# A second batch whose query factors are divided by their sums before the split, with the order of all instructions made anew

## The chip, the cores and the metric

The kernel runs on one core of a Trainium2 chip. Its metric is the device time of one execution in microseconds (us); the time before is the median of three runs. The engines are named as in the profile: PE (TensorE, matmuls) with its weight loads PEld, DVE (VectorE), ACT (ScalarE), POOL (GpSimd) and SP (SyncE, which here only issues transfers).

## What is computed

For each of 4 batches with 12608 tokens of 128 channels, 49 agents attend to the tokens (`a2k`), the tokens attend to the agents (`q2a`), and an expert network is added for the 128 tokens of a batch with the highest scores:

```python
a2k = sm(agents, k)                 # softmax(agents k^T / sqrt(128))
agent_v = a2k @ v                   # 49 x 128
q2a = sm(q, agents)                 # e / (e.sum(-1) + 1e-9), e = exp(s - max)
x = q2a @ agent_v
scores = x @ w_gate
top = the 128 highest scores of the batch
out[top] = x[top] + sigmoid(scores[top]) * (relu(x[top] @ w1) @ w2)   # w1: 128 x 1024
```

All other rows of the output are `x`.

## The kernel before

A batch is cut into 7 chunks of 15 columns of 128 tokens (the last has 9). For each chunk the kernel loads keys, values and queries by one transfer each (960 KB, 967.5 KB and 960 KB) and stores one chunk of outputs.

- Keys (`k_front`): PE multiplies agents and keys in fp32 into score banks `S` (3 of them), DVE transposes a bank into `sk` and takes its maxima `mx`. When all 7 chunks are there, `k_max` finds the batch's maxima `mb`; `k_exp` subtracts them (POOL) and takes the exponential (ACT); `v_tiles` sums with the values on PE (`av`); `v_finish` makes the fp16 weights `ws` in two halves, and `iv`, which undoes their scale.
- Queries (`q_scores`): scores as before, transposed by DVE into `sq`, with the maximum `qm` of each token. `q_exp` subtracts (POOL) and takes the exponential (ACT). `q_high` and `q_low` split it into two fp16 halves, the tile `f` (ACT, POOL). PE transposes `f` (`fT`), DVE or ACT copies that to `ft`, which is kept. PE then makes the gate scores from `ft` (`pg`), and `topk` finds the 128 rows.
- Outputs (`q_out`): PE multiplies `ft` by the two halves of `ws` into a bank `po` (4 columns at a time), and DVE, ACT or ACT and POOL bring it to `og`, which is stored. `TAIL` and `FILL` name the order in which the outputs are handed to the planner: batch 0, 1, 3, 2.
- The expert network (`expert`) runs for batches 0 to 2 as one group and for batch 3 alone. POOL gathers the rows, PE makes `qT`, `sc`, `eT`, `xT`, `xe`, the hidden layer `ph` (copied to `hT`) and the product `py`; DVE adds, and POOL scatters the rows `ey` into the output by an indirect transfer. A batch's scatter waits for all its stores.

A batch in `EARLY` is treated in another way: its exponentials are divided by their sum before they are split, so its outputs need only the constant `iv`:

```python
# q_exp, only for a batch in EARLY
nc.vector.tensor_reduce(m[:, :n], sv, axis=AX.X, op=ALU.add)
nc.scalar.activation(m[:, :n], m[:, :n], AF.Identity, scale=1.0 / FSCALE, bias=eps)
nc.vector.reciprocal(m[:, :n], m[:, :n])
# q_high, only for a batch in EARLY: one product on POOL (sq<-sq,qm a second time)
# q_out, modes A and V: for a batch in EARLY, then for another
nc.scalar.activation(o4, p3, AF.Copy, scale=d["iv"][:, 0:1])
nc.vector.tensor_scalar(o4, p3, d["iv"][:, 0:1], None, op0=ALU.mult)
nc.vector.tensor_tensor(o4, p3, rate.broadcast_to([P, nt, C]), op=ALU.mult)
# q_out, mode P: for a batch not in EARLY
nc.scalar.copy(o4, p3)
nc.gpsimd.tensor_tensor(o4, o4, rate.broadcast_to([P, nt, C]), op=ALU.mult)
```

For a batch outside `EARLY`, `q_rates` computes the rates `r` of its tokens from a third column of `pg`. `MODES` has one letter for each quarter of a chunk.

The order of the instructions is made by a planner (`place`) before anything is issued. It walks through time with a cost for each instruction, and where several are ready on an engine it takes the one with the lowest number in the table `RANKS`, less `STICK` if it is of the same kind as the last one on that engine. Each engine then works through its list in order. All instructions are issued in one place, so the profile gives them all line 1435; they are told apart by their tiles.

Of the kernel before, what the change touches and what calls it, by code (L numbers as in the profile page):

```python
# [40 lines left out]
EARLY = (0,)  # L41
MODES = ('AVAV', 'VPVP', 'VPVP', 'VPVP')
# [7 lines left out]
STICK = 6130.565386853517  # L50
# [242 lines left out]
def place(rec, urgency, slack=0.0, stick=0.0):  # L293
# [81 lines left out]
    ('setup', 0): {"ACT": -123995.537, "POOL": -226775.386, "DVE": -330989.174},  # L375
# [9 lines left out]
    ('kmax', 0): {"DVE": -300206.643, "PE": -380208.421},  # L385
    ('exp', 0, 0): {"POOL": 16775.417, "ACT": -716011.048},
    ('exp', 0, 1): {"POOL": 30570.947, "ACT": 1275522.702},
    ('exp', 0, 2): {"POOL": 35917.562, "ACT": -748687.739},
    ('exp', 0, 3): {"POOL": 36968.681, "ACT": -701284.356},
    ('exp', 0, 4): {"POOL": 100274.596, "ACT": 1572848.174},  # L390
    ('exp', 0, 5): {"POOL": -23068.358, "ACT": 2543086.262},
    ('exp', 0, 6): {"POOL": 583242.912, "ACT": 134593.062},
    ('v', 0, 0): {"SP": -505160.849},
    ('av', 0, 0): {"PE": 55332.469},
    ('v', 0, 1): {"SP": -28568.405},
    ('av', 0, 1): {"PE": 27249.223},
# [71 lines left out]
    ('qe', 1, 0): {"POOL": -369154.478, "ACT": 1570736.67},
    ('turn', 1, 0): {"PE": -325314.263, "ACT": 1886989.053},
    ('gate', 1, 0): {"PE": 38546.353},  # L470
    ('q', 1, 1): {"SP": 37927.979, "PE": 111380.947, "DVE": -12731.903},
    ('qe', 1, 1): {"POOL": -548476.653, "ACT": 255692.298},
    ('turn', 1, 1): {"PE": 209170.337, "ACT": 1551250.834},
    ('gate', 1, 1): {"PE": -375489.615},
    ('q', 1, 2): {"SP": 41692.369, "PE": -22703.96, "DVE": -11241.058},
    ('qe', 1, 2): {"POOL": -313899.94, "ACT": -1601627.448},
    ('turn', 1, 2): {"PE": -355624.568, "ACT": 955330.754},
    ('gate', 1, 2): {"PE": 620462.051},
    ('q', 1, 3): {"SP": 41757.771, "PE": 30839.917, "DVE": -227921.899},
# [5 lines left out]
    ('turn', 1, 4): {"PE": 8157.362, "ACT": 401148.205},
    ('gate', 1, 4): {"PE": -179875.682},
    ('q', 1, 5): {"SP": 43756.473, "PE": 18263.577, "DVE": 112204.08},
    ('qe', 1, 5): {"POOL": 19270.315, "ACT": 1762395.711},
    ('turn', 1, 5): {"PE": 31038.115, "ACT": 1850548.195},
    ('gate', 1, 5): {"PE": 63331.63},  # L490
    ('q', 1, 6): {"SP": 50286.516, "PE": -349161.909, "DVE": -12804.369},
# [211 lines left out]
def agent_attention_moe(ctx, tc, qT, kT, va, agT, wgb, w1, w2, consts, qs, outs, capacity):  # L703
# [810 lines left out]
```

## Time and profile before

| | |
|---|---|
| median of 3 runs | 294.15 us (293.65 to 295.35) |
| the profiled execution | 294.86 us, with a span of 293.0 us from first to last instruction |
| PE, DVE, ACT, POOL busy | 265.7 us (91%), 218.5 (75%), 169.9 (58%), 186.2 (64%) |
| moved by DMA | 106.68 MB, mean 364 GB/s |
| chain that ended last | PE 44% of the span; ACT 7%, DMA 7%, DVE 2% |

Times of the trace are counted from the span's start. Busy is the time in which an engine has an instruction under way. A releaser is the work that ended an engine's idle time. The chain of waits is followed back from the last instruction. A matmul in fp32 is recorded as two passes. A row by stretch has the stretch and its length, then each engine's busy time with its instructions in brackets, the clock granted to PE as a share of its full 2.4 GHz, the busy share of the 16 DMA engines, and what they moved.

### The profile page before, as it was taken

Reading aid. Unit: us, or ns where it says so; the run is one execution under the profiler, and the core shown is the slowest. Engines: PE = TensorE matmul, PEld = TensorE weight load, DVE = VectorE, ACT = ScalarE, POOL = GpSimd, SP = SyncE. Lnnn points to the kernel's source line nnn. Section 1 sums busy time; section 2 is a strip of 40 time slices with the busy share of each in tenths; the row PEclk is TensorE's granted clock in tenths of the full one; section 3 lists DMA queues with packets and bytes.
Section 4 is the critical chain, followed back from the end, with each engine's and each line's share of the span. In section 5 each row is a group of like instructions: output and inputs, shape, how many; then the busy total and the mean of one; then the engine's idle time right before and its main releaser. Section 6 shows DMA issues by size and latency. Waiting matters only on the chain.

```text
span 293.0 us, 8554 instructions
## 1 busy us (share of the span) xinstructions
PE 265.7 (91%) x3524; PEld 176.5 (60%) x3524; DVE 218.5 (75%) x507; ACT 169.9 (58%) x306; POOL 186.2 (64%) x158
## 2 busy tenths in 40 slices
PE   1767898998999999999999999989999999999980
PEld 0212355663676544465856356456887988999880
DVE  1799977968954999985798985768928499897520
ACT  1021355432652399968675589497998759755300
POOL 8014699357992446699522597799908475879622
PEclk9999999999999999999999999999999999999995
DMA  7999999999999999999999999999902389999971
GB/s 278 425 406 426 416 417 422 415 422 423 421 417 422 416 419 423 402 294 410 421 418 395 406 418 340 380 392 410 343 12 92 136 350 415 400 418 398 414 300 33
DMA packets 18204, 106.68 MB, mean 364 GB/s; under 512 B 2032, under 2 KB 3440, under 8 KB 18160
## 3 DMA queue, kind: packets, MB, share of 16 engines
q1 hardware_dynamic: 17760, 105.42, 89.2%
q8 instruction: 30, 0.49, 0.7%
q0 software_dynamic: 256, 0.52, 0.6%
q10 hardware_dynamic: 144, 0.13, 0.1%
q14 instruction: 14, 0.11, 0.1%
HBM read 79.85 MB, written 26.21 MB: 362 GB/s over the span
## 4 chain that ended last, share of the span: by engine, by line
PE 44%; ACT 7%; DMA 7%; DVE 2%; issue 2%; POOL 1%; POOLq 0%; DVEq 0%
PE po L1435 13%; PE S L1435 8%; PE av L1435 8%; DMA xT<-qT 7%; PE fT L1435 4%; PE ph L1435 3%; ACT gt L1435 2%; PE all L1435 2%; PE pg L1435 2%; PE py L1435 2%; ACT ft L1435 2%; ACT sq L1435 1%; POOL out L1435 1%; ACT f L1435 1%; DVE og L1435 1%
## 5 line engine op out<-in xcount | busy, mean ns | idle before, releaser
L1435 PE MATMUL S<-xT,ag_sb 128*32 128x480 f32 (+1 forms) x896 | 101.3, 560 | 16.3 <-DMA ag_sb<-agT 6.2
L1435 POOL TENSOR_TENSOR sq<-sq,qm 128x735 f32<-128x735 f32 (+1 forms) x35 | 47.8, 1366 | 54.5 <-DVE qm L1435 42.7
L1435 PEld LDWEIGHTS <-ft 128*128 128x128 f16 x1188 | 58.1, 97 | 18.3 <-issue 16.3
L1435 PEld LDWEIGHTS S<-xT,ag_sb 128*32 128x32 f32 x896 | 24.3, 110 | 54.2 <-issue 16.1
L1435 ACT COPY ft<-fT 128x896 f16<-128x896 f16 (+2 forms) x49 | 43.4, 900 | 20.3 <-PE fT L1435 20.2
L1435 PE MATMUL po<-ws,ft 128*128 128x128 f16 x792 | 53.2, 219 | 1.6 <-ACT og L1435 0.6
L1435 POOL TENSOR_TENSOR f<-sq,f 128x735 f16<-128x735 f32 (+1 forms) x28 | 42.8, 1529 | 16.1 <-issue 7.7
L1435 PE MATMUL av<-v,sk 128*64 128x129 f32 x792 | 50.5, 276 | 0.4 <-DMA v<-va 0.4
L1435 PEld LDWEIGHTS av<-v,sk 128*64 128x64 f32 x792 | 44.7, 136 | 8.8 <-issue 4.9
L1435 POOL TENSOR_TENSOR og<-og,r 128x512 f32<-128x512 f32 (+1 forms) x39 | 35.9, 941 | 20.1 <-ACT og L1435 19.9
L1435 POOL TENSOR_TENSOR sk<-sk,mb 128x735 f32<-128x735 f32 (+1 forms) x28 | 47.1, 1701 | 0.6 <-DVE rs L1435 0.6
L1435 DVE STREAM_TRANSPOSE sq<-S 128x480 f32<-128x480 f32 (+1 forms) x56 | 35.7, 645 | 14.5 <-PE S L1435 11.5
L1435 DVE STREAM_TRANSPOSE sk<-S 128x480 f32<-128x480 f32 (+1 forms) x56 | 35.6, 639 | 9.3 <-PE S L1435 7.0
L1435 DVE TENSOR_REDUCE mx<-S 128x1 f32<-128x480 f32 (+1 forms) x56 | 33.4, 607 | 5.7 <-PE S L1435 5.2
L1435 DVE TENSOR_TENSOR og<-po,r 128x512 f32<-128x512 f32 (+1 forms) x42 | 27.0, 658 | 8.5 <-PE po L1435 7.1
L1435 PEld LDWEIGHTS <-f 128*128 128x128 f16 x396 | 22.9, 98 | 13.6 <-issue 8.9
L1435 DVE TENSOR_REDUCE qm<-sq 128x15 f32<-128x735 f32 (+1 forms) x35 | 30.2, 862 | 1.1 <-ACT sq L1435 0.7
L1435 ACT ACTIVATE sq<-sq,lift 128x735 f32<-128x735 f32 (+1 forms) x28 | 25.0, 893 | 9.5 <-POOL sq L1435 9.2
L1435 PE MATMUL fT<-idh,f 128*128 128x128 f16 x396 | 28.7, 220 | 0.5 <-ACT ft L1435 0.4
L1435 ACT CAST f<-sq 128x735 f16<-128x735 f32 (+1 forms) x28 | 22.2, 794 | 11.1 <-POOL sq L1435 10.9
L1435 ACT ACTIVATE sk<-sk 128x735 f32<-128x735 f32 (+1 forms) x28 | 22.2, 797 | 10.4 <-POOL sk L1435 10.3
L1435 ACT COPY og<-po 128x512 f32<-128x512 f32 (+1 forms) x39 | 20.7, 538 | 9.4 <-PE po L1435 7.1
(131 smaller groups left out, 240.0 us busy)
## 6 DMA issues: line engine op xcount, KB each, us to landing
v<-va SPq DMA_DIRECT2D x24, 967.5 KB, 9.7
xT<-kT SPq DMA_DIRECT2D x24, 960.0 KB, 10.1
xT<-qT SPq DMA_DIRECT2D x24, 960.0 KB, 9.0
out<-og SPq DMA_DIRECT2D x24, 960.0 KB, 6.3
v<-va SPq DMA_DIRECT2D x4, 580.5 KB, 8.2
xT<-kT SPq DMA_DIRECT2D x4, 576.0 KB, 8.6
xT<-qT SPq DMA_DIRECT2D x4, 576.0 KB, 8.4
out<-og SPq DMA_DIRECT2D x4, 576.0 KB, 7.7
```

Of the source, the lines that this page charges most:

```text
L1435: call(*args, **kwargs)
```

## The change

Batch 1 joins batch 0 in `EARLY`. For each of its chunks DVE forms the sum of the exponentials, ACT adds the small constant, DVE takes the reciprocal, and POOL multiplies, all before the split. Its rates are no longer made. Its outputs go by ACT and DVE in turn, scaled by `iv`, where they went by DVE and by ACT and POOL. `STICK` is larger, and all 276 lines of `RANKS` have new numbers, so the order changes on every engine.

```diff
-EARLY = (0,)
-MODES = ('AVAV', 'VPVP', 'VPVP', 'VPVP')
+EARLY = (0, 1)
+MODES = ('AVAV', 'AVAV', 'VPVP', 'VPVP')
...
-STICK = 6130.565386853517
+STICK = 10922.517314977244
...
 RANKS = {
-    ('const', 0): {"SP": 93128.276},
...
-    ('k', 0, 0): {"SP": -558242.88, "PE": -60419.549, "DVE": -307691.923},
...
```

On PE, at the very end of its list, before the change (`py_0_796` is the product of the group of three batches, `ph_3` and `py_0_814` are batch 3's):

```order
L1435 MATMUL py_0_796<-w_end,hT_0_0_793 128x128
L1435 MATMUL ph_3_0_813<-xT_0_809,w_held 128x128 x3
L1435 MATMUL ph_3_0_813<-xT_0_809,w_end 128x128
L1435 MATMUL py_0_796<-w_held,hT_0_0_784 128x128 x2
L1435 MATMUL py_0_796<-w_held,hT_0_0_787 128x128 x2
L1435 MATMUL py_0_796<-w_held,hT_0_0_790 128x128 x2
L1435 MATMUL py_0_796<-w_held,hT_0_0_793 128x128
L1435 MATMUL py_0_796<-w_end,hT_0_0_793 128x128
L1435 MATMUL py_0_814<-w_held,hT_3_0_810 128x128 x4
L1435 MATMUL py_0_814<-w_held,hT_3_0_812 128x128 x3
L1435 MATMUL py_0_814<-w_end,hT_3_0_812 128x128
```

The same place of PE's list in the change (`py_0_795` is the group's product, `py_0_813` batch 3's):

```order
L1435 MATMUL py_0_795<-w_held,hT_0_0_783 128x128 x2
L1435 MATMUL py_0_795<-w_held,hT_0_0_786 128x128 x2
L1435 MATMUL py_0_795<-w_held,hT_0_0_789 128x128 x2
L1435 MATMUL py_0_795<-w_held,hT_0_0_792 128x128
L1435 MATMUL py_0_795<-w_end,hT_0_0_792 128x128
L1435 MATMUL xe_0_807<-wfs,ey_0_805 128x129
L1435 MATMUL ph_3_0_810<-xT_0_808,w_held 128x128 x4
L1435 MATMUL ph_3_0_812<-xT_0_808,w_held 128x128 x3
L1435 MATMUL ph_3_0_812<-xT_0_808,w_end 128x128
L1435 MATMUL py_0_813<-w_held,hT_3_0_809 128x128 x4
L1435 MATMUL py_0_813<-w_held,hT_3_0_811 128x128 x3
L1435 MATMUL py_0_813<-w_end,hT_3_0_811 128x128
```

The group's last product now ends ahead of both hidden layers of batch 3, which stood between its parts before.

On SP, rows 84 to 90 of its list before the change, the last loads (`xT_3_583` is chunk 3 of batch 3's queries, the `v` are batch 3's values, `og` a store):

```order
L1435 DMA out<-og_1_641 128x1920
L1435 DMA xT_3_583<-qT 128x1920
L1435 DMA v_0_538<-va 128x1935
L1435 DMA out<-og_0_636 128x1920
L1435 DMA v_4_543<-va 128x1935
L1435 DMA v_2_541<-va 128x1935
L1435 DMA v_1_540<-va 128x1935
```

Rows 82 to 90 of SP's list in the change (`xT_3_582` is the same chunk 3, `xT_5_600` chunk 5 of the same queries):

```order
L1435 DMA xT_6_609<-qT 128x1152
L1435 DMA w_held<-w 128x7x128
L1435 DMA xT_3_582<-qT 128x1920
L1435 DMA v_0_537<-va 128x1935
L1435 DMA out<-og_5_660 128x1920
L1435 DMA v_4_542<-va 128x1935
L1435 DMA xT_5_600<-qT 128x1920
L1435 DMA v_2_540<-va 128x1935
L1435 DMA v_1_539<-va 128x1935
```

Chunk 3 moved up by one row, and chunk 5, which was ahead of it, moved behind a store and two loads of values.

On DVE, where batch 1's queries come in, before the change (`sq_0_292` and `qm_0_296` are batch 1's chunk 0, `top` and `at` the ranking of batch 0, `S_4` and `mx_372` keys of batch 2):

```order
L1435 STREAM_TRANSPOSE sq_0_292<-S_0_1_295 128x15x32
L1435 TENSOR_REDUCE scs<-pg_171 128x99
L1435 TENSOR_REDUCE qm_0_296<-sq_0_292 128x15
L1435 MEMSET scs 64x1
L1435 STREAM_TRANSPOSE sk_4_389<-S_4_0_391 128x15x32
L1435 MAX top_226<-scs 128x8
L1435 TENSOR_REDUCE mx_372<-S_4_0_391 128x1
```

The same stage in the change (`sq_1` and `sq_2` are batch 1's chunks 1 and 2, `gt_0` is the ranking of batch 0):

```order
L1435 TENSOR_REDUCE qm_0_296<-sq_0_292 128x15
L1435 MAX top_226<-scs 128x8
L1435 STREAM_TRANSPOSE sq_2_311<-S_2_0_313 128x15x32
L1435 RECIPROCAL qm_0_296<-qm_0_296 128x15
L1435 MAX_INDEX at_0_227<-top_226,scs 128x8
L1435 STREAM_TRANSPOSE sq_2_311<-S_2_1_314 128x15x32
L1435 TENSOR_REDUCE qm_1_306<-sq_1_302 128x15
L1435 SCALAR_TENSOR_TENSOR gt_0_231,c_0_228<-all_0_230,top_226,minus_107 128x512
```

The row of `qm_0_296` shown second is the sum; it and the reciprocal now stand among the transposes that free the score banks.

## Rows read from the trace of the kernel before

**Rows 1.** By stretch, busy us: PE, PEld, DVE, ACT, POOL; clock, DMA, GB/s.

```profile
0.00:80.00 80.00, 64.34 (x738) 31.55 (x739) 63.79 (x131) 26.26 (x42) 48.57 (x45) 1.00 0.99 406
80.00:190.00 110.00, 108.83 (x1472) 65.07 (x1468) 87.24 (x204) 75.64 (x127) 69.24 (x51) 1.00 1.01 400
190.00:200.00 10.00, 8.56 (x128) 5.59 (x124) 5.78 (x10) 9.70 (x14) 9.33 (x7) 1.00 0.98 390
200.00:280.00 80.00, 79.34 (x1166) 69.89 (x1159) 60.51 (x160) 57.74 (x124) 55.09 (x54) 1.00 0.76 307
```

**Rows 2.** Pieces of the chain of waits (start us, length us, what).

```profile
129.93 1.90 PE av L1435 x30
...
140.59 5.21 PE av L1435 x90
...
157.08 0.94 PE S L1435 x8
...
182.30 10.62 DMA xT<-qT
...
193.05 1.82 PE S L1435 x16
...
260.34 9.47 PE po L1435 x168
```

**Rows 3.** The chain of waits, PE's last products.

```profile
276.83 0.42 PE xe L1435 x2
...
277.25 1.09 PE ph L1435 x8
...
281.02 1.80 PE py L1435 x16
```

**Rows 4.** Instructions in order of time at the end (start us, length us, what).

```profile
283.47 1.04 POOL L1435 DMA_INDIRECT out<-ey,idx  x1 [7.44 <-DVE ey L1435]
...
284.20 0.39 PE L1435 MATMUL py<-w_end,hT 128*128 128x128 f32 x2
...
284.63 0.35 DVE L1435 SCALAR_TENSOR_TENSOR ey<-py,g,bases 128x128 f32<-128x128 f32 x1 [0.92 <-PE py L1435]
...
287.37 0.97 POOL L1435 DMA_INDIRECT out<-ey,idx  x1 [0.30 <-issue]
```

**Rows 5.** Groups by shape (total busy us, mean ns, idle before and its releaser).

```profile
L1435 POOL TENSOR_TENSOR sq<-sq,qm 128x735 f32<-128x735 f32 x30 | 43.1, 1437 | 54.5 <-DVE qm L1435 42.7 <-PE pc L1435 9.0 <-DVE iv L1435 1.8
...
L1435 DVE TENSOR_REDUCE qm<-sq 128x15 f32<-128x735 f32 x30 | 27.2, 905 | 1.0 <-ACT sq L1435 0.7
...
L1435 DVE TENSOR_TENSOR og<-po,r 128x512 f32<-128x512 f32 x39 | 26.2, 687 | 8.5 <-PE po L1435 7.1 <-POOL og L1435 0.6 <-issue 0.2
...
L1435 POOL TENSOR_TENSOR og<-og,r 128x512 f32<-128x512 f32 x21 | 21.8, 1039 | 11.1 <-ACT og L1435 11.1
...
L1435 POOL TENSOR_TENSOR og<-og,r 128x384 f32<-128x384 f32 x18 | 14.8, 826 | 8.9 <-ACT og L1435 8.9
...
L1435 ACT COPY og<-po 128x512 f32<-128x512 f32 x21 | 12.3, 584 | 7.4 <-PE po L1435 5.0 <-POOL og L1435 1.7 <-issue 0.6
...
L1435 ACT ACTIVATE og<-po,iv 128x512 f32<-128x512 f32 x13 | 9.0, 689 | 8.4 <-PE po L1435 7.6 <-DMA out<-og 0.8
...
L1435 DVE TENSOR_SCALAR og<-po,iv 128x512 f32<-128x512 f32 x7 | 5.1, 730 | 0.3 <-PE po L1435 0.3
...
L1435 DVE RECIPROCAL qm<-qm 128x15 f32<-128x15 f32 x6 | 1.3, 213 | 0.0
```

**Rows 6.** Busy us by stretch again, columns as in rows 1.

```profile
60.00:110.00 50.00, 49.08 (x669) 29.59 (x660) 39.82 (x91) 23.98 (x42) 31.12 (x22) 1.00 1.02 420
...
210.00:240.00 30.00, 29.34 (x513) 26.33 (x508) 18.75 (x59) 25.47 (x52) 16.01 (x17) 1.00 0.38 150
```

**Rows 7.** SyncE's wait before issuing (us, times, longest), and the stores' landing.

```profile
SPq L1435 <- POOL og L1435: 29.8, 21, 2.7
...
out<-og SPq DMA_DIRECT2D x24, 960.0 KB, 6.3
```

More of the change, by code (lines that the diff above doesn't have):

```diff
@@ L485 @@
[L485 to L491, printed above, removed]
-    ('qe', 1, 6): {"POOL": -68284.931, "ACT": 1442992.742},
-    ('turn', 1, 6): {"PE": 49015.397, "ACT": 978312.709},
@@ new lines @@
+    ('kmax', 0): {"DVE": 41091.545, "PE": 58712.794},
+    ('exp', 0, 0): {"POOL": -88028.326, "ACT": 169482.5},
+    ('exp', 0, 1): {"POOL": -22401.104, "ACT": 321716.736},
+    ('exp', 0, 2): {"POOL": 70975.178, "ACT": 315931.785},
+    ('exp', 0, 3): {"POOL": 58294.679, "ACT": 304754.866},
+    ('exp', 0, 4): {"POOL": 39134.622, "ACT": 334237.156},
+    ('exp', 0, 5): {"POOL": 51140.999, "ACT": 225861.786},
+    ('exp', 0, 6): {"POOL": 55847.904, "ACT": 305110.098},
+    ('v', 0, 0): {"SP": 11990.05},
@@ new lines @@
+    ('av', 0, 0): {"PE": 42293.51},
+    ('v', 0, 1): {"SP": 20852.403},
+    ('av', 0, 1): {"PE": -95203.721},
+    ('v', 0, 2): {"SP": 25732.307},
+    ('av', 0, 2): {"PE": 48113.417},
+    ('v', 0, 3): {"SP": 26879.58},
+    ('av', 0, 3): {"PE": 36554.066},
+    ('v', 0, 4): {"SP": -154.989},
+    ('av', 0, 4): {"PE": -244316.769},
+    ('v', 0, 5): {"SP": 27655.575},
+    ('av', 0, 5): {"PE": 87914.589},
+    ('v', 0, 6): {"SP": 28400.238},
+    ('av', 0, 6): {"PE": 38896.804},
+    ('fin', 0): {"DVE": -136605.102, "PE": -175038.306, "POOL": 41207.367, "ACT": 135592.531},
@@ new lines @@
+    ('v', 1, 3): {"SP": 38724.278},
+    ('av', 1, 3): {"PE": -52626.156},
+    ('v', 1, 4): {"SP": 39890.524},
+    ('av', 1, 4): {"PE": -11759.034},
+    ('v', 1, 5): {"SP": 36195.979},
+    ('av', 1, 5): {"PE": 14422.173},
+    ('v', 1, 6): {"SP": 42755.004},
+    ('av', 1, 6): {"PE": -31267.968},
+    ('fin', 1): {"DVE": -74755.122, "PE": 14171.844, "POOL": 105161.528, "ACT": 203300.271},
+    ('q', 1, 0): {"SP": 30179.692, "PE": 72602.013, "DVE": 21920.253},
+    ('qe', 1, 0): {"POOL": 26200.37, "ACT": 37175.521, "DVE": -131176.201},
@@ new lines @@
+    ('turn', 1, 0): {"PE": 41625.788, "ACT": 299836.372},
+    ('gate', 1, 0): {"PE": 120142.116},
+    ('q', 1, 1): {"SP": 33402.969, "PE": 8366.256, "DVE": -20577.692},
+    ('qe', 1, 1): {"POOL": 51174.467, "ACT": 169449.033, "DVE": -151397.235},
+    ('turn', 1, 1): {"PE": -32284.285, "ACT": 322414.047},
+    ('gate', 1, 1): {"PE": 21998.116},
+    ('q', 1, 2): {"SP": 33807.496, "PE": -144782.77, "DVE": 51695.362},
+    ('qe', 1, 2): {"POOL": -235273.659, "ACT": 302795.625, "DVE": -139719.702},
@@ new lines @@
+    ('turn', 1, 2): {"PE": -226769.55, "ACT": 95600.617},
+    ('gate', 1, 2): {"PE": -147984.307},
+    ('q', 1, 3): {"SP": 36162.698, "PE": 97560.472, "DVE": 22293.936},
+    ('qe', 1, 3): {"POOL": -234610.212, "ACT": 620750.577, "DVE": 33342.187},
+    ('turn', 1, 3): {"PE": 93743.452, "ACT": 114030.316},
+    ('gate', 1, 3): {"PE": 104216.682},
+    ('q', 1, 4): {"SP": 38908.869, "PE": -149443.55, "DVE": -74909.023},
+    ('qe', 1, 4): {"POOL": -9485.145, "ACT": 288645.948, "DVE": 76905.944},
@@ new lines @@
+    ('turn', 1, 4): {"PE": 37408.451, "ACT": -12644.685},
+    ('gate', 1, 4): {"PE": 73954.586},
+    ('q', 1, 5): {"SP": 40977.226, "PE": 10360.343, "DVE": -24619.285},
+    ('qe', 1, 5): {"POOL": 13693.816, "ACT": -1489.582, "DVE": 140647.768},
+    ('turn', 1, 5): {"PE": 41925.35, "ACT": 176559.789},
+    ('gate', 1, 5): {"PE": 101867.087},
+    ('q', 1, 6): {"SP": 43108.967, "PE": 1987.447, "DVE": 59353.843},
+    ('qe', 1, 6): {"POOL": 7509.724, "ACT": 109581.577, "DVE": 95288.3},
+    ('turn', 1, 6): {"PE": 24728.76, "ACT": 376587.278},
@@ new lines @@
+    ('exp', 2, 6): {"POOL": 105000.47, "ACT": 300570.261},
+    ('v', 2, 0): {"SP": 52990.062},
+    ('av', 2, 0): {"PE": 55529.894},
+    ('v', 2, 1): {"SP": 62667.751},
+    ('av', 2, 1): {"PE": -152064.485},
+    ('v', 2, 2): {"SP": 67358.17},
+    ('av', 2, 2): {"PE": 53875.337},
+    ('v', 2, 3): {"SP": 72217.498},
+    ('av', 2, 3): {"PE": -59843.51},
+    ('v', 2, 4): {"SP": 72663.539},
+    ('av', 2, 4): {"PE": -33624.72},
+    ('v', 2, 5): {"SP": 74850.42},
+    ('av', 2, 5): {"PE": -33658.187},
@@ new lines @@
+    ('v', 2, 6): {"SP": 77305.048},
+    ('av', 2, 6): {"PE": 56335.979},
+    ('fin', 2): {"DVE": 152365.316, "PE": 24986.18, "POOL": -59785.981, "ACT": 615805.887},
+    ('q', 2, 0): {"SP": 53802.922, "PE": 66110.096, "DVE": 39614.828},
+    ('qe', 2, 0): {"POOL": 10740.758, "ACT": 892442.626},
+    ('turn', 2, 0): {"PE": 56713.704, "ACT": -46958.433},
+    ('gate', 2, 0): {"PE": 112176.506},
+    ('q', 2, 1): {"SP": 55658.992, "PE": 24952.713, "DVE": 59235.462},
+    ('qe', 2, 1): {"POOL": 57064.69, "ACT": 225895.253},
@@ new lines @@
+    ('turn', 2, 1): {"PE": 104183.215, "ACT": 221991.543},
+    ('gate', 2, 1): {"PE": 109266.024},
+    ('q', 2, 2): {"SP": 59815.085, "PE": 49650.94, "DVE": 6021.961},
+    ('qe', 2, 2): {"POOL": -66562.965, "ACT": -187738.301},
+    ('turn', 2, 2): {"PE": 35234.977, "ACT": 91640.625},
+    ('gate', 2, 2): {"PE": 77741.519},
+    ('q', 2, 3): {"SP": 58312.012, "PE": 43191.995, "DVE": 8139.867},
+    ('qe', 2, 3): {"POOL": -233464.489, "ACT": 21916.249},
+    ('turn', 2, 3): {"PE": 122448.379, "ACT": 179899.696},
@@ new lines @@
+    ('gate', 2, 3): {"PE": 39616.282},
+    ('q', 2, 4): {"SP": 73844.148, "PE": 62544.089, "DVE": 7122.312},
+    ('qe', 2, 4): {"POOL": 44816.234, "ACT": 3855.012},
+    ('turn', 2, 4): {"PE": 66472.533, "ACT": 222742.067},
+    ('gate', 2, 4): {"PE": 92375.268},
+    ('q', 2, 5): {"SP": 65255.993, "PE": 16519.236, "DVE": -29844.625},
+    ('qe', 2, 5): {"POOL": 40340.929, "ACT": 333307.707},
+    ('turn', 2, 5): {"PE": 23158.457, "ACT": 37208.988},
+    ('gate', 2, 5): {"PE": 69987.679},
+    ('q', 2, 6): {"SP": 69776.556, "PE": -40154.394, "DVE": 8173.335},
@@ new lines @@
+    ('exp', 3, 4): {"POOL": 98818.915, "ACT": 359355.544},
+    ('exp', 3, 5): {"POOL": 51854.827, "ACT": 181963.863},
+    ('exp', 3, 6): {"POOL": 67323.406, "ACT": 168833.049},
+    ('v', 3, 0): {"SP": 104056.363},
+    ('av', 3, 0): {"PE": 41304.235},
+    ('v', 3, 1): {"SP": 123284.333},
+    ('av', 3, 1): {"PE": 74363.156},
+    ('v', 3, 2): {"SP": 120287.105},
+    ('av', 3, 2): {"PE": -88221.877},
+    ('v', 3, 3): {"SP": 145463.798},
+    ('av', 3, 3): {"PE": 25736.185},
+    ('v', 3, 4): {"SP": 106280.547},
@@ new lines @@
+    ('av', 3, 4): {"PE": 43963.724},
+    ('v', 3, 5): {"SP": 180303.406},
+    ('av', 3, 5): {"PE": -14556.522},
+    ('v', 3, 6): {"SP": 174139.637},
+    ('av', 3, 6): {"PE": 83029.451},
+    ('fin', 3): {"DVE": -36008.362, "PE": 79111.701, "POOL": 55242.641, "ACT": 304548.35},
+    ('q', 3, 0): {"SP": 80810.207, "PE": 10586.507, "DVE": -80226.963},
+    ('qe', 3, 0): {"POOL": 53539.19, "ACT": 216528.568},
+    ('turn', 3, 0): {"PE": 26608.785, "ACT": 561091.791},
+    ('gate', 3, 0): {"PE": 94500.451},
@@ new lines @@
+    ('q', 3, 1): {"SP": 85252.717, "PE": -139385.203, "DVE": 34253.681},
+    ('qe', 3, 1): {"POOL": 75895.054, "ACT": 280728.695},
+    ('turn', 3, 1): {"PE": 24695.293, "ACT": 885886.131},
+    ('gate', 3, 1): {"PE": 60525.082},
+    ('q', 3, 2): {"SP": 77697.983, "PE": 67091.419, "DVE": -47541.597},
+    ('qe', 3, 2): {"POOL": 115584.915, "ACT": 332448.607},
+    ('turn', 3, 2): {"PE": 101309.388, "ACT": 102954.697},
+    ('gate', 3, 2): {"PE": -52500.659},
+    ('q', 3, 3): {"SP": 100636.061, "PE": 64826.475, "DVE": -141771.208},
@@ new lines @@
+    ('qe', 3, 3): {"POOL": 51764.421, "ACT": 301168.828},
+    ('turn', 3, 3): {"PE": 11825.526, "ACT": 296620.776},
+    ('gate', 3, 3): {"PE": -187523.368},
+    ('q', 3, 4): {"SP": 86742.912, "PE": 77862.341, "DVE": 31395.721},
+    ('qe', 3, 4): {"POOL": 90001.964, "ACT": 410215.634},
+    ('turn', 3, 4): {"PE": -147542.832, "ACT": 162543.555},
+    ('gate', 3, 4): {"PE": 219205.052},
+    ('q', 3, 5): {"SP": 112490.1, "PE": 50595.585, "DVE": -27764.321},
+    ('qe', 3, 5): {"POOL": 18812.867, "ACT": 181930.396},
@@ new lines @@
+    ('turn', 3, 5): {"PE": 66760.758, "ACT": 291895.213},
+    ('gate', 3, 5): {"PE": 93389.392},
+    ('q', 3, 6): {"SP": 100505.705, "PE": 69570.745, "DVE": 140681.235},
+    ('qe', 3, 6): {"POOL": 45075.642, "ACT": 374494.151},
+    ('turn', 3, 6): {"PE": 2926.386, "ACT": 175128.088},
+    ('gate', 3, 6): {"PE": 112456.633},
+    ('rank', 3): {"DVE": 48925.661, "ACT": -48158.192, "PE": 64046.929},
+    ('weights', 0): {"SP": 116778.499},
+    ('fill', 0, 0): {"PE": 48224.194, "ACT": 316266.373, "DVE": 129417.787, "SP": 67512.517},
@@ new lines @@
+    ('out', 1, 13): {"PE": 99398.7, "ACT": 153124.837, "DVE": 82913.767, "SP": 87502.362},
+    ('out', 3, 14): {"PE": 174869.758, "DVE": -22019.66, "ACT": 336032.547, "POOL": 89135.788, "SP": 42690.221},
+    ('out', 3, 15): {"PE": 99565.647, "DVE": -111257.831, "ACT": 224587.73, "POOL": 90778.515, "SP": 82613.139},
+    ('out', 3, 16): {"PE": 93209.988, "DVE": -137567.37, "ACT": 2357.117, "POOL": 55276.108, "SP": -229749.35},
+    ('out', 3, 17): {"PE": 88780.029, "DVE": -151125.37, "ACT": 302648.086, "POOL": 43998.46, "SP": 32344.14},
@@ L645 @@
+    ('expert', 2): {"POOL": 38822.733, "PE": 214325.217, "DVE": -26426.609, "ACT": 335914.832},
+    ('expert', 3): {"POOL": -240553.185, "PE": 107739.067, "DVE": -50621.084, "ACT": 308149.546},
 }
```

315 lines of the change are left out of this document (84 added, 231 removed), and 58 rows, old and new, of the table RANKS.

## The prediction

> **What bounds the kernel now.** I read the busy times by stretch first. In [rows 1] the reader is to see TensorE (PE) at 64.34 of the first 80 us, then at 108.83 of 110, 8.56 of 10 and 79.34 of 80: 15.66 us of idle time before 80 us, and only 1.17 + 1.44 + 0.66 = 3.27 us in the 200 us behind. The clock column stays at 1.00 there, which is the upper of the two levels, 2.4 GHz. VectorE (DVE) has 63.79 of the first 80 us, and the DMA engines are full up to 200 us. So the kernel starts up on loads and DVE, and from 80 us on PE sets the pace.
>
> Busy PE might still be slow PE, so I looked at the chain of waits next. [Rows 2] has 168 passes of the output products in 9.47 us, 56.4 ns for 128 columns, and a chunk of scores (16 passes) in 1.82 us. At 2.4 GHz 128 columns alone take 53.3 ns, so the stretch is real work at its rate. The same rows show the one late wait: a load of query chunk that takes 10.62 us to come, up to 192.9 us, and PE's scores behind it. That is where the idle 1.44 us of 190 to 200 us sits.
>
> Last I read the end in order of time. [Rows 3] and [rows 4] show the third product of the expert group of three ending at 281.02 + 1.80 = 282.82 us, PE's last matmul at 284.20 + 0.39 = 284.59 us, and four scatters on GpSimd (POOL), the first at 283.47, the last at 287.37, so 1.30 us apart. The span ends at 293.0, 5.6 us behind the start of the last scatter. Nothing else runs there.
>
> **The change part by part.** PE multiplies the same tiles, and the bytes moved are the same. The engines beside it get other work, at the prices of [rows 5]:
>
> - DVE gets a sum over each of the seven query chunks of batch 1, at most 7 x 0.905 = 6.3 us, and 7 reciprocals of 0.213 us, 1.5 us: 7.8 us at most. Its share of the outputs (14 products with the rate at 0.687 us at most, for 13 scalings at 0.730 us or less) comes out even within 0.6 us.
> - ScalarE (ACT) scales 14 pieces at 0.689 us where it copied 13 at 0.584 us, about 2 us more.
> - POOL loses 7 x 1.039 + 6 x 0.826 = 12.2 us of products in the output stage, and gains at most 7 x 1.437 = 10.1 us in the query stage of batch 1.
>
> POOL's 12.2 us I cost at nothing: between 200 and 280 us PE idles 0.66 us in all [rows 1], so what waits for POOL there is covered by PE's own queue. What it might free is a rival below.
>
> *The end.* In the order of the change all three products of the group of three stand ahead of the last 34 passes: two of xe, 16 of ph and 16 of batch 3's py. Their time in [rows 3] is 0.42 + 1.09 + at most 1.09 + 1.80 = 4.2 to 4.4 us. Before, only batch 3's own py stood there. The first scatter came 283.47 - 282.82 = 0.65 us after the group's products; three of them take 3.9 us, so they are through 0.2 to 0.4 us after PE's end. The last scatter needs batch 3's product on DVE, which ended 284.63 + 0.35 - 284.59 = 0.39 us after PE. It can start about 0.4 us after PE's end, where it started 287.37 - 284.59 = 2.78 us after. That is -2.4 us. I take -2.1: with nothing between ph and py, PE may wait some tenths for the two activations. The other cover is the last store. Its products end some 10 us ahead of PE's end, and a store lands 6.3 us after its issue [rows 7], so it should be there. Were it not, the gain falls towards nothing: bounds 0 and -2.4.
>
> *The late load.* The load that made PE wait stands on SyncE's queue at row 85 with three stores and every other query load ahead of it. In the change it is row 84, with one load fewer ahead (960 KB at the 400 GB/s of [rows 1] is 2.4 us), and PE's printed rows ahead of its scores, at the durations of [rows 2], are the same work within 1 us. That would end the idle 1.44 us. But the query load that it passed, chunk 5, is now behind another store at row 88. I take -1.0, bounds 0 and -1.44.
>
> *The changes of kind on PE.* Counted over PE's printed rows, one kind of matmul follows another 241 times before and 224 times after. What one costs shows in two places of [rows 2]: half a chunk of scores takes 0.94 us where a whole one takes 1.82, so a cut costs 0.06 us, and 30 passes of av take 1.90 us where 90 take 5.21 (1.74 for 30), 0.16 us. Bounds 0 and -17 x 0.16 = -2.7. I take -1.0, 17 times the cut in the scores, which is the kind cut most often.
>
> *DVE in the stage of batches 0 to 2.* The 7.8 us are added where DVE is already full: 39.82 of 50 us from 60 to 110 us [rows 6]. There the new order also puts one chunk more of keys. The 10.2 us that are free cover the sum, but not at each moment: a sum that stands in DVE's queue ahead of a score transpose holds a score bank, and PE's next scores wait for it. Bounds: 0, if the free time takes it all, and +7.8, if none. I take +1.0, near the lower end, since PE shows almost no wait in a stretch where DVE is 80% busy.
>
> *The first 80 us.* The 15.66 us stay: of the first 17 transfers on SyncE's queue that carry scores both orders have the same number, 13, so PE is fed alike. I take 0, within half a us either way.
>
> The sum is -2.1 - 1.0 - 1.0 + 1.0 = -3.1 us. The profiled execution took 294.86 us (a span of 293.0 and 1.9 around it), so 291.8. That execution lies 0.7 us above the median of the runs, 294.15; against that median I expect 291.0.
>
> Of the gauges themselves: the Trainium skill, Perfetto Trace Analysis, Identifying the Most-Contended Engine, says that matmul busy time is a poor measure of how near PE is to its roof, and that for DMA the use of memory bandwidth is to be read. The page's table (Engine Utilization) gives 358 GB/s for a core. By that rule this kernel, at 364 GB/s over its span, is bound by its bytes, which the change leaves alone, and the sum would be 0. The trace does not agree: 406 GB/s in the first 80 us is above that figure, and between 210 and 240 us the engines move 150 GB/s [rows 6] while PE is full.
>
> **The rivals.** *Slower, DVE takes PE's place.* From about 60 to 160 us DVE does batch 1's sums, batch 0's ranking and the scores of two batches. For it: the added 7.8 us and the extra chunk of keys nearly fill the idle 10.2 us [rows 6], and DVE works in order. Against it: from 110 us on its queue lightens, and PE has other kinds of work to put between. It decides from where DVE has no free time left in 60 to 110 us; then the whole 7.8 us land on PE, and the time is 294.15 + 7.8 - 3.1 in gains = about 298.9; with 5 us of it, 296.
>
> *No change.* The gains at the late load and in the changes of kind are lost in other waits, and the end is held by the last store or by a scatter of another batch: 294.2, within a us. For it: the transfers are full for 200 us and their bytes stay. Against it: the end of PE's queue is plain to see.
>
> *Much faster, the stores come free of POOL.* SyncE waited 29.8 us, 21 times, for POOL's products before it could issue a store [rows 7], 1.42 us each. The seven stores of batch 1 no longer do: 7 x 1.42 = 9.9 us, in the very stretch where the DMA engines are at 38% [rows 6]; then 284.2. Against it: a store that goes out sooner ends nothing unless PE too ends sooner, and PE is full there.
>
> **How the numbers follow.** I give the forecast 0.56, no change 0.24, DVE 0.15, the stores 0.05. The forecast alone ranges from 288.5 to 293.0: with the end and the changes at their best and DVE at nothing, about -5.5; with the end at its -2.1 and DVE eating most of the rest, about -1. The range is 288.0 to 296.0: it takes in no change and the milder half of DVE's case, and leaves the stores' case and the harder half of DVE's outside. Half a percent, 1.5 us, is about what a measurement of this kernel can tell from none. Faster than 292.7: 0.51 of the forecast, 0.05 of the stores, 0.02 of no change, 0.58. Slower than 295.6: 0.13 of DVE and 0.03 of no change, 0.16. Between: 0.26.
>
> **What would show it.** The end is right if the last scatter starts within 1 us of PE's last matmul, and three of the four lie before that matmul's end. The late load is right if PE's idle time from 80 to 280 us falls below 2.5 us. DVE's cost shows as PE waiting for DVE's transposes or maxima between 60 and 160 us, with DVE above 9.5 of every 10 us. The forecast is wrong if PE's last matmul ends later than 285.6 us in the span, whatever the scatters do, or if the last scatter waits for a transfer. If PE's end comes before 281 us, the gain was in the middle and I have mis-sized it.

## The result, and the profile after

The changed kernel takes 289.54 us (median of 6 runs, 288.92 to 291.2) where the kernel before took 293.92 us beside it (6 runs, 293.64 to 295.35): a ratio of 0.984, with a 95% interval of 0.982 to 0.987. That is 4.4 us less; 3.1 us were forecast. Executions that took over 1.5% longer than the fastest of the same kernel are left out of every ratio here: one of the changed kernel at 335.99 us, one of the kernel before at 340.23 us and two of experiment e8 at 291.5 and 291.82 us.

The profiled executions lie further apart than the medians: 294.86 us before, 289.3 us after, with spans of 293.0 and 287.4 us. One pair of traces thus shows some 1.2 us more than the kernels differ by, and what follows uses it for places, and the timed experiments for sizes.

Busy times by stretch of the changed kernel, columns as in [rows 1], which the first four answer; the last two answer [rows 6]:

```profile
0.00:80.00 80.00, 66.55 (x782) 31.83 (x782) 64.22 (x131) 27.39 (x46) 48.23 (x46) 0.98 0.99 407
80.00:190.00 110.00, 109.63 (x1450) 65.25 (x1449) 93.94 (x218) 80.40 (x138) 85.51 (x60) 0.98 1.01 413
190.00:200.00 10.00, 9.87 (x155) 7.29 (x150) 6.43 (x14) 8.71 (x13) 9.05 (x7) 1.00 1.01 384
200.00:280.00 80.00, 78.94 (x1129) 70.22 (x1129) 59.37 (x155) 54.49 (x118) 38.07 (x39) 1.00 0.76 305
...
60.00:110.00 50.00, 49.96 (x692) 31.36 (x690) 44.02 (x105) 31.67 (x61) 38.76 (x29) 1.00 1.01 410
210.00:240.00 30.00, 29.05 (x471) 25.52 (x468) 19.00 (x51) 21.28 (x43) 9.55 (x9) 1.00 0.48 196
```

PE's idle time from 80 to 280 us is 0.37 + 0.13 + 1.06 = 1.56 us (3.27 before). DVE's 39.82 of 50 us became 44.02, and PE's matmuls show no wait for DVE from 80 to 190 us; its weight loads, which overlap with matmuls, wait 4.0 us for DVE's `sq` there (1.7 us before). POOL has 38.07 us from 200 to 280 us where it had 55.09. Between 210 and 240 us the stores run at 196 GB/s instead of 150.

The end of the changed kernel in order of time, which answers [rows 4]:

```profile
278.28 1.04 POOL L1435 DMA_INDIRECT out<-ey,idx  x1 [5.23 <-DVE ey L1435]
...
279.63 0.98 POOL L1435 DMA_INDIRECT out<-ey,idx  x1 [0.30 <-issue]
...
280.91 0.97 POOL L1435 DMA_INDIRECT out<-ey,idx  x1 [0.30 <-issue]
281.56 0.39 PE L1435 MATMUL py<-w_end,hT 128*128 128x128 f32 x2
281.99 0.35 DVE L1435 SCALAR_TENSOR_TENSOR ey<-py,g,bases 128x128 f32<-128x128 f32 x1 [2.14 <-PE py L1435]
283.16 0.97 POOL L1435 DMA_INDIRECT out<-ey,idx  x1 [1.28 <-DMA out<-og]
```

PE ends at 281.95 us (284.59 before). Three scatters start ahead of that, and the fourth starts 1.21 us behind it, where it started 2.78 us behind. Its releaser is now a store. The chain of waits says which (start us, length us, what):

```profile
270.42 2.63 POOL og L1435 x3
...
273.07 9.32 DMA out<-og
...
283.45 0.67 POOL out L1435
```

The chain no longer ends in PE's products, as in [rows 3]. It runs through POOL's products for the last output chunk, the store issued when they are done, and its 9.32 us of transfer. DVE's `ey` ends at 282.34 us and the store at 282.39 us, so the two are nearly level: an earlier `ey` alone would end nothing sooner, and an earlier store alone at most 0.5 us (e10 below). The three other scatters go out before this store lands, and a scatter waits for all stores of its batch, so the late store is one of batch 3, whose scatter is the last in line.

### The profile page after: what moved, and what is told of

It reads as the page before. It is cut to its first block, busy times and chain, and to the rows that moved or that the text cites. A ratio compares the mean times of both kernels' runs of the same rounds, so it can differ in the third digit from the quotient of the medians.

```text
span 287.4 us, 8559 instructions
## 1 busy us (share of the span) xinstructions
PE 266.9 (93%) x3524; PEld 176.3 (61%) x3524; DVE 224.3 (78%) x517; ACT 171.6 (60%) x313; POOL 183.4 (64%) x152
## 4 chain that ended last, share of the span: by engine, by line
PE 65%; POOL 12%; DMA 9%; ACT 7%; DVE 3%; issue 3%; POOLq 0%; ACTq 0%
PE S L1435 24%; PE av L1435 13%; PE po L1435 13%; PE fT L1435 6%; POOL sk L1435 5%; DMA xT<-kT 4%; DMA out<-og 3%; POOL f L1435 3%; PE pg L1435 2%; PE all L1435 2%; ACT gt L1435 2%; PE ph L1435 2%; POOL sq L1435 2%; DMA ag_sb<-agT 2%; ACT ft L1435 2%
## 5 line engine op out<-in xcount | busy, mean ns | idle before, releaser
L1435 PE MATMUL S<-xT,ag_sb 128*32 128x480 f32 (+1 forms) x896 | 102.4, 572 | 10.8 <-DMA ag_sb<-agT 6.0
L1435 POOL TENSOR_TENSOR sq<-sq,qm 128x735 f32<-128x735 f32 (+1 forms) x42 | 56.9, 1368 | 34.9 <-DVE qm L1435 27.8
L1435 PEld LDWEIGHTS <-ft 128*128 128x128 f16 x1188 | 59.1, 98 | 15.1 <-issue 13.3
L1435 POOL TENSOR_TENSOR f<-sq,f 128x735 f16<-128x735 f32 (+1 forms) x28 | 42.7, 1527 | 23.5 <-ACT f L1435 21.2
L1435 PEld LDWEIGHTS S<-xT,ag_sb 128*32 128x32 f32 x896 | 23.5, 111 | 54.1 <-issue 24.6
L1435 PE MATMUL av<-v,sk 128*64 128x129 f32 x792 | 49.9, 275 | 0.4 <-DMA v<-va 0.4
L1435 DVE TENSOR_REDUCE qm<-sq 128x15 f32<-128x735 f32 (+1 forms) x42 | 36.1, 865 | 1.2 <-ACT sq L1435 0.7
L1435 POOL TENSOR_TENSOR og<-og,r 128x512 f32<-128x512 f32 (+1 forms) x26 | 24.3, 944 | 14.1 <-ACT og L1435 13.9
L1435 ACT ACTIVATE sk<-sk 128x735 f32<-128x735 f32 (+1 forms) x28 | 22.4, 799 | 12.4 <-POOL sk L1435 12.2
L1435 ACT ACTIVATE og<-po,iv 128x512 f32<-128x512 f32 (+1 forms) x28 | 18.0, 663 | 12.6 <-PE po L1435 11.5
L1435 DVE SCALAR_TENSOR_TENSOR gt<-all,top,minus 128x512 bf16<-128x512 f32 x32 | 23.6, 739 | 0.9 <-PE all L1435 0.5
```

Source lines behind the costliest of these rows:

```text
L1435: call(*args, **kwargs)
```

## The experiments

Each was timed against the kernel before on the same chip: e1 to e4 on one chip, e5 to e8 on a second, e9 to e12 on a third. Differences in us between two experiments are differences of their ratios times 294 us, with both intervals in them. The changed kernel was run again among them, as e5:

> The changed kernel once more, unchanged, beside the experiments. Both theories: 289 to 291 us, ratio to before 0.982 to 0.988; the experiments on the changed kernel are read against it.

Measured: 290.42 us, ratio 0.9855 (0.9824 to 0.9887). It is the mark against which the experiments on the changed kernel are read.

**e1: the end undone in the changed kernel** (the lists rearranged after the planner):

```diff
+    put(order, g[1], after=pick(order, "PE", "ph0_3_0")[0])
+    put(order, g[2], after=up)        # up: the second ph of batch 3
+    for x in ey: put(order, x, before=last)
```

> The changed kernel with TensorE's end put back in the order of before: of the three products py of the group, the second stands behind the first ph of batch 3 and the third behind the second ph; the additions ey stand behind them. Nothing else is moved. If the order of the end is a term of the gain (theory 1), all four scatters come one after another again after TensorE's last matmul: the last starts at about 286.2 us instead of 283.2, and the time rises by 2.1 to 3.0 us to 291.6 to 292.5 (ratio to before 0.992 to 0.995). If the last store's transfer, which the last scatter waits for in the changed kernel, sets the end whatever the order is (rival), the time stays at 289.5 to 290.0 (ratio 0.985 to 0.987).

Measured: 293.35 us, ratio 0.998 (0.995 to 1.0009), 3.7 us (2.4 to 4.9) slower than e5. Its end in order of time:

```profile
274.83 0.49 PE L1435 MATMUL xT<-ey,wfs 49*128 49x128 f32 x2 [0.38 <-DVE ey L1435]
275.70 0.49 PE L1435 MATMUL xe<-wfs,ey 49*128 49x129 f32 x2 [0.38 <-DVE xT L1435]
...
283.14 0.39 PE L1435 MATMUL py<-w_end,hT 128*128 128x128 f32 x2
...
286.31 0.97 POOL L1435 DMA_INDIRECT out<-ey,idx  x1 [0.30 <-issue]
```

The scatters stand in line again, the last at 286.31 us. And PE now stops twice for DVE, 0.38 us each. In the changed kernel the group's products lie between `eT`, `xT` and `xe`, and neither stop is there:

```profile
273.26 1.73 PE L1435 MATMUL py<-w_held,hT 128*128 128x128 f32 x14
...
275.14 0.49 PE L1435 MATMUL xT<-ey,wfs 49*128 49x128 f32 x2
...
275.56 1.83 PE L1435 MATMUL py<-w_held,hT 128*128 128x128 f32 x14
...
277.54 0.49 PE L1435 MATMUL xe<-wfs,ey 49*128 49x129 f32 x2
```

So the end's order is worth at least its term in the changed kernel, and the rival falls. All the rest of the change, with the end undone, is only 0.6 us (-0.3 to 1.5) under the kernel before.

**e2: the end alone, in the kernel before** (the same moves the other way; the scatter of batch 2 goes ahead of batch 3's):

```diff
+    put(order, g[1], after=g[0])
+    put(order, g[2], after=g[1])
+    put(order, ey[0], before=set_)    # set_: the copy of xe to bases
```

> The kernel before with the end of the changed kernel alone: the three products py of the group stand together ahead of xe, the two ph and the py of batch 3; the additions ey and the scatters follow in the changed kernel's order. Theory 1 (the end's order is worth its term by itself): 2.1 to 3.0 us less than before, 290.9 to 291.8 us (ratio 0.990 to 0.993). Rival (the last store's transfer, or a scatter that waits for it, takes the place of the scatters in line): 293.4 to 293.9 (ratio 0.998 to 1.000).

Measured: 294.69 us, ratio 1.0013 (0.9988 to 1.0038): nothing. The third scatter of its trace shows why:

```profile
282.03 0.98 POOL L1435 DMA_INDIRECT out<-ey,idx  x1 [0.30 <-issue]
...
286.54 0.97 POOL L1435 DMA_INDIRECT out<-ey,idx  x1 [3.53 <-DMA out<-og]
287.81 0.97 POOL L1435 DMA_INDIRECT out<-ey,idx  x1 [0.30 <-issue]
```

The last store, one of batch 2, is still under way, and batch 3's scatter stands behind the one that waits. Part of the loss is my placing: with batch 3's scatter first, the last would have started at 286.54, still only 0.83 us before 287.37. In the changed kernel the late store is batch 3's, so it holds back only the scatter that comes last anyway. The rival holds here.

**e6: the same with shorter stores** (the last four stores cut):

```diff
+        x.calls = [(call, (args[0][:, :7], args[1][:, :7]), kwargs)]
```

> The kernel before with the changed kernel's end (as e2_end_alone, which gained nothing) and, besides, only the first 7 columns of each of the last four output chunks stored (1.3 MB or 3.2 us of transfer at 410 GB/s are left out). Theory 2 (in e2 the last store's transfer, for which the third scatter waited until 286.5 us, had taken the place of the scatters in line): with the transfers out of the way the end's order pays, 2 to 3 us less than before, 291.0 to 292.1 us (ratio 0.990 to 0.993). Rival (the end's order is worth nothing, or TensorE's later end in e2 ate it): 293.5 to 294.5 us (ratio 0.998 to 1.002).

Measured: 293.05 us, ratio 0.9953 (0.9927 to 0.9979), 1.8 us (0.7 to 2.8) under e2. Its scatters no longer wait for a store:

```profile
282.96 0.97 POOL L1435 DMA_INDIRECT out<-ey,idx  x1 [0.37 <-issue]
...
284.59 0.97 POOL L1435 DMA_INDIRECT out<-ey,idx  x1 [0.67 <-DVE ey L1435]
```

That is 1.4 us (0.6 to 2.1) under the kernel before: theory 2's direction with about half its size, and clear of the rival's range. The end's order pays where the last store is early. The shorter stores without the new end were not run; in the trace of before no scatter waits for a store (the last one follows the others in line, [rows 4]), which speaks against a gain by them alone.

**e4: POOL's work given back to the changed kernel's output stage:**

```diff
+        by = kwargs["scale"].unsqueeze(2).broadcast_to(list(o4.shape))
+        x.calls = [(call, (o4, p3, form), {}), (mul, (o4, o4, by), {"op": ALU.mult})]
```

> The changed kernel with POOL's work in the output stage given back: the first and third part of every output chunk of batch 1 are copied by ScalarE and then multiplied in place by the same constant on POOL (about 13 us more on POOL), in the changed kernel's order. If POOL's work there lies beside TensorE's (the prediction counted its loss at nothing): 289.0 to 290.1 us (ratio 0.983 to 0.987). Rival (the gain comes from stores that no longer wait for POOL): most of the gain goes, 291.5 to 293.5 us (ratio 0.992 to 0.999).

Measured: 291.47 us, ratio 0.9917 (0.9884 to 0.9949), 1.8 us (0.5 to 3.2) slower than e5: clear of the first theory's range, and at the near end of the rival's. The end of its chain of waits:

```profile
269.69 2.39 POOL og L1435 x3
...
272.48 3.62 POOL og L1435 x4
...
276.11 9.03 DMA out<-og
...
286.20 0.67 POOL out L1435
```

POOL works through its outputs late, so the last store goes out at 276.11 us instead of 273.07, and the last scatter comes 2.75 us later. So POOL's relief has a value: its queue sets when the last store leaves.

**e10: shorter last stores in the changed kernel** (the cut of e6 in the changed kernel):

> The changed kernel with only the first 7 columns of each of the last four output chunks stored (2.1 MB, 5.1 us of transfer at 410 GB/s are left out). If the last scatter's wait for the last store is all that the transfers still hold at the end: it starts right after the last ey, 0.8 us sooner, ratio to before 0.981 to 0.984. Rival A (that wait costs nothing): 0.985 to 0.987. Rival B (the stores hold TensorE too, by buffers that come free late): 2 us or more, 0.972 to 0.979.

Measured: 289.11 us, ratio 0.983 (0.9777 to 0.9883), 0.7 us under e5 with 1.8 us either way: open by time. In its trace the last scatter starts 0.28 us after `ey` (0.82 us in the changed kernel), so at most 0.5 us hang on the store there. Rival B is not seen.

```profile
281.51 0.35 DVE L1435 SCALAR_TENSOR_TENSOR ey<-py,g,bases 128x128 f32<-128x128 f32 x1 [2.14 <-PE py L1435]
282.14 0.97 POOL L1435 DMA_INDIRECT out<-ey,idx  x1 [0.73 <-DVE ey L1435]
```

**e3: the late load brought forward in the kernel before:**

```diff
+    for name in ("w2_held", "w1_held"):
+        put(order, pick(order, "SP", name)[0], after=late)   # late: chunk 3 of batch 3's queries
```

> The kernel before with the two loads w_held (0.9 MB) moved on the transfer queue behind the load xT that came late at 190 to 193 us. The load then has 0.9 MB less ahead of it and lands some 2 us sooner. Theory 1 (TensorE's stop there is a loss of its own): 0.8 to 1.4 us less, 292.5 to 293.1 us (ratio 0.995 to 0.997). Rival (the transfers are the bound of that stage, so the same bytes in another order end at the same time, or the next wait takes the stop over): 293.6 to 294.2 us (ratio 0.999 to 1.001).

Measured: 294.26 us, ratio 1.002 (0.9995 to 1.0046). The edit did its part, PE is busy for 9.96 of the 10 us where it had 8.56 [rows 1], but the time stays:

```profile
190.00:200.00 10.00, 9.96 (x151) 6.82 (x152) 7.69 (x15) 9.98 (x15) 10.00 (x7) 1.00 1.02 420
```

So the stop was no loss of its own, as far as the times can tell. What took it over is not shown: the one trace is of the fastest of the 12 executions (292.81 us).

**e7 and e8: less work for PE in the middle, then fewer loads as well:**

```diff
+            order.remove(pick(order, "PE", "av_", tag=("av", b, c))[2])
...
+            x.calls = [(call, (args[0][:, :10 * 129], args[1][:, :10]), kwargs)]   # e8 only
```

> The changed kernel with 60 of the multiplications av of batches 1 and 2 left out (the last 5 of 15 of 12 chunks; about 58 ns each, 3.5 us of TensorE between 80 and 200 us), all loads as they are. If TensorE's own work is the bound of that stage (the prediction's view): 3.0 to 3.5 us less than the changed kernel, ratio to before 0.972 to 0.976. If the transfers are the bound there (theory 2): 0 to 0.8 us less, ratio 0.982 to 0.986.

> As e7_less_matmul, and the columns of v that are no longer used are not loaded (60 columns of 66 KB, 4.0 MB, 9.6 us of transfer at 413 GB/s). If TensorE's work is the bound between 80 and 200 us: the same as e7_less_matmul within 0.5 us. If the transfers are the bound there (theory 2): 3 us or more under e7_less_matmul, down to where TensorE binds again, ratio to before 0.965 to 0.975.

Measured: e7 287.8 us, ratio 0.9772 (0.9743 to 0.9801), 2.4 us (1.2 to 3.7) under e5; e8 a ratio of 0.9791 (0.9744 to 0.9839), no better than e7. The edit is twice as large as its expectation has it: a multiplication in fp32 is two passes, so 60 of them are 120 passes of some 60 ns. The changed kernel's passes, then e7's, and e7's busy times from 80 to 190 us:

```profile
L1435 PE MATMUL av<-v,sk 128*64 128x129 f32 x792 | 49.9, 275 | 0.4 <-DMA v<-va 0.4
...
L1435 PE MATMUL av<-v,sk 128*64 128x129 f32 x672 | 42.5, 276 | 0.7 <-DMA v<-va 0.5
```

```profile
80.00:190.00 110.00, 104.72 (x1356) 59.29 (x1355) 93.79 (x218) 81.43 (x140) 86.05 (x61) 1.00 1.02 416
```

Of 7.4 us taken from PE only 2.4 came through, and PE, which idled 0.37 us in this stretch, idles 5.28. So PE's work counts there, but with little to spare: behind a gain of some 2 us other waits take over. One of them is on POOL, whose `f` PE awaits for 2.9 us from 80 to 200 us (0.3 us in the changed kernel). It is not the transfers, though the DMA engines show 1.02: 4.0 MB of loads less gave nothing on top, where theory 2 wanted 3 us. By the reading of the Trainium skill that the prediction weighed (Perfetto Trace Analysis, Identifying the Most-Contended Engine) the bytes would bind; e8 does not agree.

**e9: what normalises batch 1, left out:**

```diff
+        for x in pick(order, "DVE", f"qm_1_{c}", **own) + pick(order, "ACT", f"qm_1_{c}", **own):
+            order.remove(x)
+        order.remove(pick(order, "POOL", f"sq_1_{c}", **own)[1])
```

> The changed kernel with what normalises batch 1's query factors left out (7 sums and 7 reciprocals on VectorE, 7.8 us, 7 small operations on ScalarE and 7 multiplications on POOL, about 10 us), all else in the changed kernel's order; its outputs are thus not the reference's. The prediction's term for VectorE (+1.0 us, bounds 0 to +7.8): 1.0 us less than the changed kernel or more, ratio to before 0.979 to 0.982. Rival (the added work lies wholly beside TensorE's): no change, ratio 0.984 to 0.987.

Measured: 289.74 us, ratio 0.9833 (0.9782 to 0.9883), 0.6 us under e5 with 1.8 us either way. The theories are not told apart, but most of the 7.8 us is hidden: DVE's busy time from 80 to 190 us fell from 93.94 to 87.78 us for at most 2.4 us.

```profile
80.00:190.00 110.00, 108.76 (x1447) 64.85 (x1450) 87.78 (x204) 77.44 (x130) 75.03 (x52) 1.00 1.01 407
```

**e11 and e12: the normalisation without new numbers (the diff), and the third batch too** (`EARLY = (0, 1, 2)` and a third `'AVAV'` in the changed kernel):

```diff
-EARLY = (0,)
-MODES = ('AVAV', 'VPVP', 'VPVP', 'VPVP')
+EARLY = (0, 1)
+MODES = ('AVAV', 'AVAV', 'VPVP', 'VPVP')
```

> The kernel before with batch 1 normalised ahead of the split and its outputs scaled by a constant, and the numbers that set the order left as they were in before. Theory 1 (the gain is one of the order, the normalisation gives only what POOL's relief in the output stage is worth): 292.5 to 295 us, ratio 0.994 to 1.002. Rival (the normalisation itself carries the gain): ratio 0.984 to 0.990.

> The changed kernel with batch 2 normalised ahead of the split as well (EARLY = (0, 1, 2), its outputs scaled by a constant on ScalarE and VectorE), the numbers that set the order left alone: VectorE has 7.8 us more ahead of 200 us, POOL some 12 us less after it. If VectorE's sums stay hidden and POOL's relief is worth what e4 showed (1 to 2 us): ratio to before 0.977 to 0.983. Rival (VectorE, at 9 of 10 between 110 and 130 us, becomes the bound, or the order, made for other work, loses more): 0.988 to 1.003.

Measured: e11 327.72 us, ratio 1.111 (1.105 to 1.117); e12 320.98 us, ratio 1.090 (1.084 to 1.097). Both were far slower than any theory had it. Three stretches of e11, and its longest wait on POOL (us, times, longest):

```profile
100.00:120.00 20.00, 15.50 (x157) 8.01 (x153) 19.09 (x47) 10.46 (x23) 11.11 (x8) 0.91 0.98 393
...
220.00:240.00 20.00, 15.31 (x170) 10.03 (x171) 10.11 (x26) 16.31 (x32) 12.71 (x9) 0.92 0.50 164
...
260.00:280.00 20.00, 15.22 (x217) 14.48 (x215) 13.59 (x41) 11.45 (x31) 3.71 (x4) 0.74 0.35 143
```

```profile
POOL sq L1435 <- DVE qm L1435: 67.2, 20, 12.2
```

PE loses 4.5 us or more in each of these stretches. Only in the first is DVE full; in the other two it has 6 to 10 us free, and the engines wait for each other in line. POOL waits 67.2 us for DVE's `qm`, against 27.8 us in the changed kernel and 42.7 us before [rows 5]. The old table has no number for DVE's work in `q_exp` of batch 1, so the planner takes zero, behind most of DVE's other work for that batch; for batch 2 in e12 the changed kernel's table has none either. That the missing number is what costs the time is argued from this wait and not tested. e11 is thus the normalisation with its sums unplaced, not the best old order. The other half, the new numbers on the old arithmetic, was not tried.

## Why the prediction was right, and where its steps were not

The direction and the range were right, and the size was 1.3 us short. By its steps:

- *The end, -2.1.* Its check was met in part: three of four scatters start ahead of the end of PE's last matmul, but the last starts 1.21 us behind it, not within 1 us, and it waits for a transfer, which the prediction named as a sign that the forecast is wrong. As `ey` was nearly level with that store, the wait costs at most 0.5 us (e10). The mechanism was right and its size too small: undoing it costs 3.7 us (2.4 to 4.9, e1), in part through two waits of PE for DVE that the order also covers. What the step had not sized is its condition. It took the last store to "be there", at the median landing of 6.3 us; at the end a store takes 9.0 to 9.3 us. In the kernel before, where the late store holds batch 2's scatter with batch 3's behind it, the same order of PE gains nothing (e2), and 1.4 us with shorter stores (e6). The step's lower bound, 0, was for that case.
- *POOL's relief, at nothing.* This step failed. "What waits for POOL there is covered by PE's own queue" does not hold for the last chunk: the last store leaves when POOL's queue lets it, and some 13 us more on POOL make the kernel 1.8 us slower (e4). The rival that the stores come free of POOL had the engine right and the stores wrong. SyncE's waits for POOL did fall from 29.8 us [rows 7] to 11.4 us, but its waits for DVE's `og` rose from 22.4 to 51.1 us (first row below: before; then the changed kernel), and what the chain of waits shows to count is the last store.

```profile
SPq L1435 <- DVE og L1435: 22.4, 15, 6.5
...
SPq L1435 <- DVE og L1435: 51.1, 21, 10.2
SPq L1435 <- POOL og L1435: 11.4, 10, 1.9
```

- *The late load, -1.0.* The stop went, as forecast, and PE's idle time fell below 2.5 us. But e3 takes the same stop out of the kernel before and gains nothing (at best 0.15 us by its interval). The term was not a gain by itself.
- *Changes of kind, -1.0.* Not isolated. PE's own time counts in the middle only up to some 2 us (e7), so 17 fewer changes may be worth something; how much is open.
- *DVE, +1.0.* Within what was seen: e9 bounds the whole normalisation of the inputs at some 2.4 us. DVE rose to 44.02 of 50 us and PE stayed full.
- *The rival "DVE takes PE's place".* It did not happen in the changed kernel. With the old numbers, which leave the sums unplaced, the same arithmetic costs 33 us (e11), so the change as made needs its new order; whether a few numbers would do was not tried.

What the runs bear out is the end together with an early last store. With the end undone, 0.6 us of the gain is left (e1); with the end alone, nothing is gained (e2). POOL's 1.8 us act through the same last store, so they are not to be added to the 3.7. For the late load, the changes of kind and DVE, together -1.0 us in the sum, e1's 0.6 us are the nearest measure, with whatever its two added waits of PE hide. That the sum came within 1.3 us of the result is in part luck: the end was too small, POOL's part was left out, and the late load, which gains nothing alone, made up for some of it.

## What to carry to other kernels

At the end of a kernel, follow every chain into the last instruction: the product, the store it has to wait for, and the engine that feeds that store. Moving one of two level chains shows nothing until the other is moved too, so an edit that gains nothing alone (e2) may be the larger part of a pair. Where a planner sets the order, new work needs its place in the table before it can be judged. And price an edit by the passes that the trace counts: 60 multiplications were 120 passes.

## What the runs showed of the hardware

PE's granted clock fell in the midst of the kernel in some executions. The trace of before does not show it ahead of the end. In the changed kernel PE was busy for 5.02 of the 10 us up to 30 us, and in the next 5 us the mean clock was 0.66; in e5 (second fence) it was at 0.50, which is the lower level, 1.2 GHz, for all of 30 to 35 us:

```profile
20.00:30.00 10.00, 5.02 (x53) 1.50 (x49) 8.54 (x18) 3.17 (x5) 5.85 (x4) 1.00 1.01 418
30.00:35.00 5.00, 4.72 (x27) 1.40 (x31) 4.39 (x10) 0.94 (x2) 3.42 (x3) 0.66 1.03 429
...
185.00:190.00 5.00, 5.00 (x55) 2.23 (x52) 4.21 (x6) 4.52 (x6) 5.00 (x4) 0.66 1.02 419
```

```profile
25.00:30.00 5.00, 2.90 (x16) 0.61 (x16) 2.31 (x5) 1.74 (x2) 3.97 (x3) 0.73 1.02 419
30.00:35.00 5.00, 3.50 (x17) 0.76 (x17) 4.17 (x10) 1.13 (x2) 2.09 (x2) 0.50 1.02 426
35.00:40.00 5.00, 5.00 (x38) 1.49 (x34) 3.89 (x7) 1.03 (x2) 4.71 (x4) 0.75 1.01 419
```

The second fall of the changed kernel, behind 185 us, followed a run of 69 small gate products and a wait of PE for POOL (in order of time):

```profile
177.68 1.01 PE L1435 MATMUL S<-xT,ag_sb 128*32 128x480 f32 x8
...
182.11 1.98 PE L1435 MATMUL pg<-ws,ft 128*128 128x3 f16 x69
...
184.81 0.75 PE L1435 MATMUL fT<-idh,f 128*128 128x128 f16 x8 [0.30 <-POOL f L1435]
...
186.34 1.83 PE L1435 MATMUL S<-xT,ag_sb 128*32 128x480 f32 x8
```

Eight passes of scores take 1.83 us there, where they take 1.01 us ahead of the fall. What PE did before a fall does not settle whether the clock falls. e7 and e9, with the changed kernel's order, were busy for 5.09 and 5.02 of the 10 us up to 30 us and kept 1.00 in the next 5. Nor does the fall belong to the new order: e2 and e3, with the old one, show 0.83 from 20 to 30 us. What it costs in time is not shown either. Of e5's executions the profiled one, at a mean clock of 0.975, took 293.01 us, and five others, at 0.986 to 0.999, took 289.33 to 291.07 us; but among the six of the result the one at 0.982 took 289.3 us and the one at 1.00 took 290.3 us.
